# Order of the first operations of an attention-and-experts block: mixing weights, mask, table and gate rows

## The chip, the cores and the metric

The kernel runs on one core of a Trainium2 chip (trn2). A core has TensorE (matrix products, into PSUM), VectorE, ScalarE and GpSimd (elementwise work; each takes its instructions in order), and SyncE (SP), whose queue issues the transfers of this kernel. The metric is the time of one execution on the device, in microseconds (us). A profiled execution beside it gives the trace.

## What is computed

Three parts in a row, all in float32; the inputs are random and some are scaled. Cut to what matters:

```python
def _attn_ref(q, k, v, s):               # 4 batches, 8 heads, 576 rows, 64 wide
    cum = np.cumsum(np.maximum(s, 0.0), axis=-1)
    bias = -(cum[:, :, :, None] - cum[:, :, None, :])
    scores = np.where(causal, -1e9, q @ k.T / 8 + np.minimum(bias, 0.0))
    return softmax(scores) @ v

def _moe_ref(x, mu_k, mu_r, w_k, w_v, w_r):
    x_prev = shift(x)                    # the row before, zero for the first
    xk = mu_k * x + (1.0 - mu_k) * x_prev
    xr = mu_r * x + (1.0 - mu_r) * x_prev
    v = np.maximum(xk @ w_k, 0.0) ** 2 @ w_v
    return v / (1.0 + np.exp(-(xr @ w_r)))

def _moe2_ref(x, w_in, g_ln, w_sg, b_sg, w_out):
    u, v = split(gelu(x @ w_in))
    v_s = np.einsum('ts,bsd->btd', w_sg, layernorm(v) * g_ln) + b_sg
    return x + (u * v_s) @ w_out
```

## The kernel before

Attention goes in 20 jobs. A job is a pair of heads; the first batch's four pairs are cut into jobs 0 to 3 (query blocks 0 to 2) and 4 to 7 (blocks 3 and 4), all later pairs are one job each. Jobs 0 to 5 use the inputs in float32; later ones are split into two float32r halves. For each block a score product (`scores`, L344) goes to PSUM; VectorE (`fold`, L361, one custom instruction and one that reads its accumulator, nm) adds the mask, scales and finds the minimum; ScalarE makes the exponential (L387). In `rows` the result is transposed by TensorE (L422), copied by ScalarE (L424) and multiplied with v (L426, L430). The first block of each job (p0) has its own path: GpSimd multiplies it by the reciprocal of its sums (L438), TensorE transposes it (L440), ScalarE copies it (L442), TensorE multiplies it (L444). The finished heads stand in the tiles xt.

The second part (`moe1`) mixes each row with the row before: ScalarE multiplies by mu1, which is 1 - mu (L594), VectorE adds mu times the row (L600), ScalarE rounds to xh (L70) and GpSimd makes the rest xl (L73). The products with w_k, w_r and w_v follow (L661). Those weights come as raw 64-bit words and are converted on the chip (`convert`): ScalarE takes the absolute value (L110), VectorE does four integer steps (L114 to L117), ScalarE rounds (L70), VectorE makes the low half (L73). Eight parts of w_k, four of w_r and eight of w_v (512 KB each) are loaded, at most five ahead of their conversion; a load is held back by a small VectorE copy (L100) that stands for the buffer of an earlier conversion. The third part, after attention and the experts, is products with w_in, w_sg and w_out.

What sets the order: the program is written as generators that interleave the steps, with priorities (`tc.cur_priority`, lower goes first; FIRST, SECOND and THIRD move the beginning ahead), and a scheduler of the Tile framework turns priorities and its own estimate of times into one fixed order for each engine. On the chip the engines then follow their orders and wait for semaphores. A transfer of SP's queue stands in that order too.

At the beginning stand: the load of s (s_sb), the running sum cum (L264, L266), its copies into the extra rows of the first operand tile qk[0] (L269 to L272), constant rows of qk[0] and qk[1] (`rest`, L155), 14 matmuls of a tile of ones (L243), the identity (`make_identity`) and the mask (L250 to L263; mask0 is its form for p0), the rows cur for the other jobs (L277, L278), and gt, the float32r form of those rows, written to gate_d in DRAM for jobs 6 and later (L286 to L298). cur, gt and others live in the pool `cum`, which closes after gt; the tiles xt and the raw w_v are allocated behind that and may lie on its memory. The mixing weights come last:

```python
    mu_sb = const.tile([P, 2, 4], F32, name="mu_sb")
    nc.sync.dma_start(mu_sb, mu)
    mu1 = const.tile([P, 2, 4], F32, name="mu1")
    nc.gpsimd.tensor_scalar(mu1, mu_sb, -1.0, 1.0, ALU.mult, ALU.add)
```

Of the kernel before, what the change touches and what calls it, by code (L numbers as in the profile page):

```python
# [18 lines left out]
B, H, S, D = 4, 8, 576, 64  # L19
# [4 lines left out]
P = 128  # L24
NEG = -1.0e9
QS = [0, 64, 192, 320, 448]
QM = [64, 128, 128, 128, 128]
KN = [64, 192, 320, 448, 576]
PTW = 1408
C0, RATE, LEAD, AHEAD = 0.7, 1.1, 0.0, 5  # L30
FIRST = 100000
WARM = 14
SPLIT = 1
# [5 lines left out]
E1, ND, SECOND, THIRD = 2, 2, 5000, 1000  # L39
PA, PC, PM, PX = -1000, -500, -500, -500  # L40
NS, NV = 6, 8
PACE = 3
N0 = 8
ENG0 = {"qh": "DA", "ql": "P", "kh": "A", "kl": "D", "vh": "DA", "vl": "P"}
ENG = {"ia": "D", "mx": "D", "ca": "D", "p0": "P", "cl": "D", "qh": "D", "ql": "P", "kh": "A", "kl": "P", "vh": "A", "vl": "P", "xh": "A", "xl": "P", "fh": "D", "fl": "P", "rs": "D", "bh": "A", "bl": "D", "nh": "D", "nl": "D", "gh": "A", "gl": "D"}
MD = 320
# [5 lines left out]
def block_kernel(ctx: ExitStack, tc: tile.TileContext, qkv, vb, s, w_r, w_k, w_v, mu, w_in, w_out, w_sgT, g_ln, b_sg, out):  # L52
# [6 lines left out]
    nc = tc.nc  # L59
# [15 lines left out]
    const = ctx.enter_context(tc.tile_pool(name="const", bufs=1))  # L75
# [60 lines left out]
    ps_m = ctx.enter_context(tc.tile_pool(name="ps_m", bufs=2, space=PSUM))  # L136
# [10 lines left out]
    qk = [None, None]  # L147
# [6 lines left out]

    def rest(x, a, b, eng):  # L155

        eng.memset(qk[x][D:, 0, a:b], 8.0)
        nc.gpsimd.memset(qk[x][D:, 1, a:b], 0.0)
        nc.gpsimd.memset(qk[x][D : D + 1, 1, a:b], -8.0)

# [72 lines left out]
    gate_d = dram.tile([48, 2, 4, S], F32, name="gate_d")  # L233
    cur_d = dram.tile([48, S], F32, name="cur_d")
    cpool = tc.tile_pool(name="cum", bufs=1)
    cp = cpool.__enter__()
    if WARM:

        ones = cp.tile([P, 512], BF16, name="ones")
        nc.vector.memset(ones, 1.0)  # L240
        pm = ps_m.tile([P, 512], F32, tag="m", name="warm")
        for _ in range(WARM):
            nc.tensor.matmul(pm, ones[:, 0:P], ones, start=True, stop=True)  # L243
    zer = cp.tile([48, S], F32, name="zer")
    nc.gpsimd.memset(zer, 0.0)
    rest(0, S - KN[2], S + KN[2], nc.vector)
    rest(1, S - KN[2], S + KN[2], nc.vector)
    ident = const.tile([P, P], F32, name="ident")
    make_identity(nc, ident)
    mask = const.tile([P, 2 * MD + P], F32, tag="mask", name="mask")  # L250
# [9 lines left out]
    )  # L260
    mask0 = const.tile([P, P], F32, name="mask0")
    nc.vector.tensor_copy(mask0, mask[:, MD : MD + P])
    nc.vector.memset(mask0[D:, 0:D], 8.0 * NEG)  # L263
    nc.vector.tensor_scalar(s_sb, s_sb, 0.0, None, ALU.max)  # L264
    cum = cp.tile([48, S], F32, name="cum")
    nc.vector.tensor_tensor_scan(cum, s_sb, zer, 0.0, ALU.add, ALU.add)  # L266
    for i in (2, 1, 0):
        a, b, o = QS[i], KN[i], S - KN[i]
# [3 lines left out]
    nc.scalar.copy(qk[0][96:97, 1, S : S + KN[2]], cum[32:33, 0 : KN[2]])  # L272
    tc.cur_priority += FIRST - SECOND
    cur = cp.tile([48, S], F32, name="cur")
    for i in range(5):
# [4 lines left out]
    for x in range(2):  # L280
        for a, b in ((0, S - KN[2]), (S + KN[2], 2 * S)):
            rest(x, a, b, nc.gpsimd)
    for c in range(max(1, E1), AHEAD):
        load_words(wk, c % 4, c // 4, after=cur)
    tc.cur_priority += SECOND - THIRD
    gt = cp.tile([48, 2, 4, S], F32R, name="gt")  # L286
# [12 lines left out]
    cpool.__exit__(None, None, None)  # L299
    tc.cur_priority += THIRD  # L300


    mu_sb = const.tile([P, 2, 4], F32, name="mu_sb")
    nc.sync.dma_start(mu_sb, mu)
    mu1 = const.tile([P, 2, 4], F32, name="mu1")
    nc.gpsimd.tensor_scalar(mu1, mu_sb, -1.0, 1.0, ALU.mult, ALU.add)

    xtp = ctx.enter_context(tc.tile_pool(name="xtp", bufs=2))
    w1b = tc.tile_pool(name="w1b", bufs=1)
# [5 lines left out]
    def prepare(n, j):  # L315
        w = jobs[n]
        q, k, v = lds.pop((n, j))
        e = ENG0 if n < N0 else ENG
        if q is not None:
# [487 lines left out]
    for size in moe1():  # L807
# [17 lines left out]
        if att is None and w2 is None:  # L825
# [207 lines left out]
```

## Time and profile before

| | us |
|---|---|
| median of 3 runs | 714.64 (714.37 to 714.86) |
| profiled execution, whole | 712.34 |
| its span | 710.5 |
| TensorE busy | 670.2 (94%) |
| VectorE busy | 510.2 (72%) |
| ScalarE busy | 407.8 (57%) |
| GpSimd busy | 231.4 (33%) |

The span is what the trace shows, from the first instruction to the last; 1.8 us of the profiled execution lie around it. The granted clock is TensorE's, as a share of its full 2.4 GHz; 0.50 is the lower level of 1.2 GHz. The profile names PE (TensorE), PEld (its weight loads), DVE (VectorE), ACT (ScalarE), POOL (GpSimd), SP (SyncE). A busy time is an average over the stretch that it stands for.

### The profile page before, as it was taken

The numbers are of one execution on the slowest core, as the hardware profiler recorded it, in microseconds if no ns is written. First come the engines' busy times: TensorE is split into PE (matmuls) and PEld (weight loads), VectorE is DVE, ScalarE is ACT, GpSimd is POOL, SyncE is SP. The second block draws the span as 40 slices with busy tenths as digits, with TensorE's granted clock in tenths as the row PEclk, the third lists the DMA queues.
The fourth block names the chain that finished last, engine by engine and source line by source line (L and its number), as shares of the span: only waits on it lengthen the run. The fifth ranks groups of instructions, "written<-read, shape, count | busy, mean of one in ns | idle before, by whom it ended". The sixth has DMA issues, their size and how long they took to land.

```text
span 710.5 us, 12931 instructions
## 1 busy us (share of the span) xinstructions
PE 670.2 (94%) x4594; PEld 630.0 (89%) x4594; DVE 510.2 (72%) x1225; ACT 407.8 (57%) x978; POOL 231.4 (33%) x234
## 2 busy tenths in 40 slices
PE   6879979998999979999989999999999999999998
PEld 3657879987999969998989999999998998998998
DVE  8869998877878688779678598852946664664643
ACT  5759776877988867797777453633433133133120
POOL 7013553546655763576463073030000000000000
PEclk8779976999999999999999999999999999999999
DMA  9884542345244332424200630004230400300101
GB/s 242 238 253 145 155 123 56 95 125 159 73 128 141 89 107 57 143 85 119 89 22 21 204 131 29 6 18 142 78 117 3 131 3 5 129 1 5 63 1 68
DMA packets 39832, 67.48 MB, mean 95 GB/s; under 512 B 6908, under 2 KB 23400, under 8 KB 39736
## 3 DMA queue, kind: packets, MB, share of 16 engines
q1 hardware_dynamic: 39768, 66.66, 31.5%
q8 instruction: 36, 0.59, 0.3%
q14 instruction: 28, 0.23, 0.1%
HBM read 51.85 MB, written 10.19 MB: 87 GB/s over the span
## 4 chain that ended last, share of the span: by engine, by line
PE 71%; ACT 10%; DVE 10%; issue 3%; DMA 3%; POOL 1%; SPq 1%; DVEq 0%; ACTq 0%; POOLq 0%
PE m L661 25%; PE pu L674 7%; PE po L674 7%; PE av L511 3%; PE t L526 3%; PE pg L912 2%; PE pg L913 2%; ACT pr L387 2%; PE pg L911 2%; PE s L346 2%; PE av L430 2%; PE pv L848 2%; PE pv L849 2%; PE pv L850 2%; PE s L347 2%
## 5 line engine op out<-in xcount | busy, mean ns | idle before, releaser
L387 ACT ACTIVATE pr<-pr,nm 128x448 f32<-128x448 f32 (+4 forms) x144 | 85.3, 593 | 19.0 <-DVE nm L361 15.4
L73 POOL TENSOR_TENSOR xl<-xf,xh 128x288 fp32r<-128x288 f32 x64 | 69.0, 1091 | 79.5 <-ACT xh L70 40.5
L661 PE MATMUL m<-xh,wk 128*128 128x288 f32 x512 | 82.6, 300 | 0.0
L661 PE MATMUL m<-kh,wv 128*128 128x288 f32 x512 | 79.8, 297 | 0.0
L361 DVE CUSTOM_DVE_ANT_0 pr<-s,mask 128x288 f32<-128x288 f32 (+4 forms) x144 | 64.0, 454 | 15.6 <-PE t L526 6.4
L661 PEld LDWEIGHTS m<-xh,wk 128*128 128x128 f32 x512 | 73.0, 191 | 0.8
L661 PEld LDWEIGHTS m<-kh,wv 128*128 128x128 f32 x512 | 71.7, 188 | 0.5
L346 PE MATMUL s<-qk 128*128 128x288 f32 (+4 forms) x144 | 47.4, 330 | 12.2 <-DVE nh L361 7.7
L600 DVE SCALAR_TENSOR_TENSOR xf<-xt,mu_sb,xf 128x288 f32<-128x288 f32 x64 | 43.8, 688 | 12.4 <-ACT xf L594 12.2
L70 ACT CAST xh<-xf 128x288 fp32r<-128x288 f32 (+1 forms) x80 | 36.3, 482 | 24.2 <-DVE xf L600 13.5
L530 DVE TENSOR_TENSOR ptl<-t,pth 128x512 fp32r<-128x512 f32 (+1 forms) x72 | 44.1, 617 | 6.3 <-ACT pth L529 5.9
L661 PE MATMUL m<-xl,wk 128*128 128x288 f32 x256 | 48.1, 303 | 0.0
L594 ACT ACTIVATE xf<-xt,mu 128x288 f32<-128x288 f32 x64 | 33.9, 536 | 24.4 <-POOL xl L73 17.8
L529 ACT CAST pth<-t 128x512 fp32r<-128x512 f32 (+1 forms) x72 | 37.8, 532 | 15.6 <-PE t L526 15.0
L73 POOL TENSOR_TENSOR qk<-qld,qk 64x576 fp32r<-64x576 f32 (+1 forms) x28 | 38.9, 1389 | 20.3 <-DVE qk L70 4.3
L347 PE MATMUL s<-qk 128*128 128x288 f32 (+4 forms) x144 | 44.7, 313 | 0.0
L661 PE MATMUL m<-kl,wv 128*128 128x288 f32 x256 | 44.1, 299 | 0.0
L622 ACT ACTIVATE kf<-m 128x288 f32<-128x288 f32 x64 | 25.9, 410 | 30.6 <-PE m L661 28.9
L346 PEld LDWEIGHTS s<-qk 128*128 128x128 f32 x144 | 28.0, 194 | 16.4 <-DVE nh L361 9.1
L661 PE MATMUL m<-xh,wr 128*128 128x288 f32 x256 | 41.0, 301 | 1.3 <-ACT rt L635 1.0
L674 PE MATMUL pu<-xh,wi 128*128 128x288 f32 x256 | 40.6, 295 | 0.2 <-ACT ut L874 0.2
L70 ACT CAST gh<-gf 128x288 fp32r<-128x288 f32 x32 | 13.9, 435 | 46.0 <-DVE gf L918 46.0
(296 smaller groups left out, 1861.4 us busy)
## 6 DMA issues: line engine op xcount, KB each, us to landing
kld<-qkv SPq DMA_DIRECT2D x28, 288.0 KB
qld<-qkv SPq DMA_DIRECT2D x24, 288.0 KB
x_d<-rt SPq DMA_DIRECT2D x8, 576.0 KB
xf<-x_d SPq DMA_DIRECT2D x8, 576.0 KB
outT<-ot SPq DMA_DIRECT2D x32, 144.0 KB
vld<-qkv SPq DMA_DIRECT2D x24, 160.0 KB
qk<-qk SPq DMA_DIRECT2D x24, 144.0 KB
rb<-rd SPq DMA_DIRECT2D x24, 128.0 KB
```

Source lines behind the costliest of these rows:

```text
L70: nc.scalar.copy(dst, src) if eng == "A" else nc.vector.tensor_copy(dst, src)
L73: (nc.gpsimd if pick(engines) == "P" else nc.vector).tensor_tensor(dst, a, b.bitcast(F32), ALU.subtract)
L346: nc.tensor.matmul(dst, qk[0][:, 0, qs], qk[0][:, 1, ks], start=True, stop=False)
L347: issued[0] = nc.tensor.matmul(dst, qk[1][:, 0, qs], qk[1][:, 1, ks], start=False, stop=True)
L361: nc.vector.tensor_tensor_reduce(out=dst, in0=src, in1=msk, scale=-0.125, scalar=first, op0=ALU.add, op1=ALU.min, accum_out=acc)
L387: i = nc.scalar.activation(dst, dst, AF.Exp, bias=nm[:, col : col + 1], scale=-1.0, accum_out=w.sm[:, col : col + 1])
L529: nc.scalar.copy(pth[:, cols], bank[:, 0:o])
L530: nc.vector.tensor_tensor(ptl[:, cols], bank[:, 0:o], pth[:, cols].bitcast(F32), ALU.subtract)
L594: nc.scalar.mul(xf, xp, mu1[:, j, c : c + 1])
L600: nc.vector.scalar_tensor_tensor(xf, xc, mu_sb[:, j, c : c + 1], xf, ALU.mult, ALU.add)
L661: i = nc.tensor.matmul(dst, w(x, c, m), xx[:, c], start=(n + c == 0), stop=(n == 2 and c == w.nk - 1))
L674: nc.tensor.matmul(dst, w(x, c, m), xx[:, c], start=(n + c == 0), stop=(n == 2 and c == w.nk - 1))
```

## The change

The load of mu_sb is issued behind the first two loads of w_k, ahead of the rest of the program's beginning; mu1 stays where it was. The tiles xt get their memory before the pool `cum`. The memset matmuls are 18 with 384 columns instead of 14 with 512; their tile of ones is a constant. A one-column exponential of ones is ScalarE's first operation, so that its table is loaded there. `rest` takes the engine for its low rows as an argument: for the first columns of qk[0] that is VectorE, for all others GpSimd. The mask is made ahead of the identity and of qk[1]'s rows; mask0 comes after the first rows of cum. The priority of gt is later by GT = 300 than the code around it, and no longer earlier by THIRD.

```diff
-WARM = 14
+WARM = 18
+GT = 300
-    def rest(x, a, b, eng):
+    def rest(x, a, b, eng, low):
         eng.memset(qk[x][D:, 0, a:b], 8.0)
-        nc.gpsimd.memset(qk[x][D:, 1, a:b], 0.0)
-        nc.gpsimd.memset(qk[x][D : D + 1, 1, a:b], -8.0)
+        low.memset(qk[x][D:, 1, a:b], 0.0)
+        low.memset(qk[x][D : D + 1, 1, a:b], -8.0)
...
+    mu_sb = const.tile([P, 2, 4], F32, name="mu_sb")
+    nc.sync.dma_start(mu_sb, mu)
+    xtp = ctx.enter_context(tc.tile_pool(name="xtp", bufs=2))
     cpool = tc.tile_pool(name="cum", bufs=1)
...
+    ones = const.tile([P, 384], BF16, name="ones")
+    nc.vector.memset(ones, 1.0)
+    idle = ps_m.tile([P, 512], F32, tag="m", name="warm")
+    for _ in range(WARM):
+        nc.tensor.matmul(idle[:, 0:384], ones[:, 0:P], ones, start=True, stop=True)
+    first = const.tile([P, 1], F32, name="first")
+    nc.scalar.activation(first, ones[:, 0:1], AF.Exp)
...
-    rest(0, S - KN[2], S + KN[2], nc.vector)
-    rest(1, S - KN[2], S + KN[2], nc.vector)
-    ident = const.tile([P, P], F32, name="ident")
-    make_identity(nc, ident)
+    rest(0, S - KN[2], S + KN[2], nc.vector, nc.vector)
     mask = const.tile([P, 2 * MD + P], F32, tag="mask", name="mask")
...
-    mask0 = const.tile([P, P], F32, name="mask0")
-    nc.vector.tensor_copy(mask0, mask[:, MD : MD + P])
-    nc.vector.memset(mask0[D:, 0:D], 8.0 * NEG)
+    ident = const.tile([P, P], F32, name="ident")
+    make_identity(nc, ident)
+    rest(1, S - KN[2], S + KN[2], nc.vector, nc.gpsimd)
...
-    tc.cur_priority += SECOND - THIRD
+    tc.cur_priority += SECOND + GT
     gt = cp.tile([48, 2, 4, S], F32R, name="gt")
...
-    tc.cur_priority += THIRD
-    mu_sb = const.tile([P, 2, 4], F32, name="mu_sb")
-    nc.sync.dma_start(mu_sb, mu)
+    tc.cur_priority -= GT
```

The scheduler moves more than the diff says, as the orders of the two programs show (the number behind a name is a buffer's; in the changed kernel lines stand one or two further down). SP's queue from the loads of w_r to those of job 4 (qk 64x2x576), before:

```order
L101 DMA wr10w<-w_r 128x512
L208 DMA vld<-qkv 128x320 x2
L304 DMA mu_sb<-mu 128x8
L101 DMA wr20w<-w_r 128x512
L189 DMA qk_86<-qkv 64x2x576
L192 DMA qk_86<-cur_d 1x576
L193 DMA qk_86<-cur_d 1x576
L204 DMA vb<-vb 128x640
L189 DMA qk_86<-qkv 64x2x576
L192 DMA qk_86<-cur_d 1x576
L193 DMA qk_86<-cur_d 1x576
L101 DMA wr30w<-w_r 128x512
```

There mu_sb is behind the two loads of v (vld). SP's queue near its beginning now:

```order
L102 DMA wk00w<-w_k 128x512
L102 DMA wk10w<-w_k 128x512
L237 DMA mu_sb<-mu 128x8
L190 DMA qk_87<-qkv 64x2x320
L205 DMA vb<-vb 128x384
```

The load of mu_sb (L304 before, L237 now) stands behind the second of w_k. From wr10w on SP's queue reads now:

```order
L102 DMA wr10w<-w_r 128x512
L304 DMA gate_d<-gt 16x4608
L190 DMA qk_87<-qkv 64x2x320
L193 DMA qk_87<-cur_d 1x576
L194 DMA qk_87<-cur_d 1x576
L304 DMA gate_d<-gt 16x4608
L102 DMA wr20w<-w_r 128x512
L102 DMA wr30w<-w_r 128x512
L190 DMA qk_86<-qkv 64x2x576
L193 DMA qk_86<-cur_d 1x576
L194 DMA qk_86<-cur_d 1x576
L205 DMA vb<-vb 128x640
```

Both writes of gate_d (L304 now) stand here, the loads of v earlier, and the load of wr30w ahead of job 4's. GpSimd, from the reciprocal's users of jobs 0 and 1 (pr, L438 before and L440 now) to the first xl, before:

```order
L356 MEMSET sm 128x16
L438 TENSOR_SCALAR pr_305<-pr_305,rc 128x128
L356 MEMSET sm 128x16
L306 TENSOR_SCALAR mu_199<-mu_sb 128x8
L438 TENSOR_SCALAR pr_418<-pr_418,rc 128x128
L73 TENSOR_TENSOR xl<-xf,xh 128x288
L356 MEMSET sm 128x16
L73 TENSOR_TENSOR xl<-xf,xh 128x288
L438 TENSOR_SCALAR pr_542<-pr_542,rc 128x128
```

There mu1 (mu_199) is between the multiplies of jobs 1 and 2. GpSimd now, behind the memsets of gt:

```order
L295 MEMSET gt 48x576
L296 MEMSET gt 48x576
L309 TENSOR_SCALAR mu_208<-mu_sb 128x8
L440 TENSOR_SCALAR pr_219<-pr_219,rc 128x128
L358 MEMSET sm 128x16
L74 TENSOR_TENSOR xl<-xf,xh 128x288
L440 TENSOR_SCALAR pr_311<-pr_311,rc 128x128
L358 MEMSET sm 128x16
L440 TENSOR_SCALAR pr_424<-pr_424,rc 128x128
```

mu1 (mu_208 now) stands ahead of job 0's multiply, and the first xl ahead of job 1's. VectorE, behind the copies of cum (L269, L271), before:

```order
L271 COPY qk_86<-cum 1x320
L278 COPY cur<-cum 16x576
L100 COPY wk20w<-cur 48x1
L100 COPY wk30w<-cur 48x1
L100 COPY wk01w<-cur 48x1
L292 CAST gt<-cur 48x576
L114 TENSOR_SCALAR cvt<-cvt 128x512
L294 TENSOR_TENSOR gt<-cur,gt 48x576
L115 TENSOR_SCALAR cvt<-cvt 128x512
L262 COPY mask_142<-mask 128x128
L361 ISA pr_89,nm<-s,mask 128x320
L361 ISA nm 128x1
```

There the copy of the mask and the first fold (L361) come last. VectorE now, behind the same copies:

```order
L274 COPY qk_86<-cum 1x320
L278 COPY mask_164<-mask 128x128
L284 COPY cur<-cum 16x576
L279 MEMSET mask_164 64x64
L363 ISA pr_89,nm<-s,mask 128x320
L363 ISA nm 128x1
L363 ISA pr_88,nm<-s,mask 128x192
L363 ISA nm 128x1
L101 COPY wk20w<-cur 48x1
L101 COPY wk30w<-cur 48x1
L101 COPY wk01w<-cur 48x1
```

The first score's fold (L361 before, L363 now) stands ahead of the small copies, gt and the first conversion step. ScalarE keeps both absolute values (L110; wk00w and wk10w) and one cast of gt ahead of its first exponential. TensorE's order differs up to about the third of its instructions and is the same from there on.

## Rows read from the trace of the kernel before

**Rows 1.** The page, busy tenths in 40 equal slices of the span, and granted clock.

```profile
PE   6879979998999979999989999999999999999998
...
PEclk8779976999999999999999999999999999999999
```

**Rows 2.** Busy us by stretch (stretch, its length, engines with instruction counts, clock, DMA share, GB/s).

```profile
12.00:26.00 14.00, 12.32 (x46) 9.31 (x45) 12.20 (x41) 9.13 (x27) 2.94 (x14) 0.52 0.92 236
26.00:38.00 12.00, 8.69 (x53) 6.45 (x52) 10.72 (x41) 8.62 (x27) 0.85 (x2) 0.99 0.90 282
38.00:42.00 4.00, 0.15 (x2) 0.00 (x0) 0.77 (x4) 1.34 (x4) 0.77 (x2) 0.74 0.96 269
42.00:50.00 8.00, 7.76 (x29) 6.82 (x30) 6.00 (x22) 6.37 (x21) 2.33 (x4) 0.50 0.92 252
50.00:98.00 48.00, 42.02 (x286) 37.25 (x285) 47.09 (x114) 40.59 (x94) 21.55 (x21) 0.96 0.50 154
98.00:118.00 20.00, 17.34 (x77) 16.05 (x75) 19.53 (x39) 13.38 (x29) 10.55 (x8) 0.50 0.33 90
118.00:138.00 20.00, 20.00 (x155) 19.84 (x155) 16.03 (x40) 15.02 (x42) 10.03 (x12) 0.99 0.33 85
138.00:710.00 572.00, 555.19 (x3939) 531.42 (x3938) 388.94 (x912) 307.55 (x727) 171.44 (x145) 1.00 0.25 77
```

**Rows 3.** The chain of waits, 31 to 43 us: start us, us, what.

```profile
31.27 9.11 issue
...
40.43 0.21 POOL mu L306
...
41.10 0.52 ACT xf L594
...
42.23 0.45 PE t L440
```

**Rows 4.** Waits from 36 to 44 us: engine, line, waited for, us, times, longest.

```profile
POOL mu L306 <- DMA mu_sb<-mu: 9.2, 1, 9.2
ACT xf L594 <- POOL mu L306: 4.7, 1, 4.7
PEld t L440 <- POOL pr L438: 4.2, 1, 4.2
...
DVE xf L600 <- ACT xf L594: 3.6, 1, 3.6
```

**Rows 5.** Timeline around 40 us: start us, us, instruction, idle before and releaser.

```profile
36.22 0.43 SPq L304 DMA_DIRECT2D mu_sb<-mu  x1
...
37.66 0.49 PE L344 MATMUL s<-qk 128*128 128x128 f32 x2 [0.48 <-DVE nm L361]
...
43.55 0.80 POOL L73 TENSOR_TENSOR xl<-xf,xh 128x288 fp32r<-128x288 f32 x1 [2.36 <-ACT xh L70]
```

**Rows 6.** Timeline of the first 12 us.

```profile
1.59 1.26 DVE L157 MEMSET qk<- 64x640 f32 x2 [0.19 <-issue]
...
5.36 1.28 ACT L270 ACT_TABLE_LOAD   x1 [5.36 <-DVE cum L266]
...
6.34 1.58 POOL L159 MEMSET qk<- 1x640 f32 x2
...
10.74 0.67 ACT L110 ACTIVATE cvt<-wk10w 128x512 f32<-128x512 f32 x1 [0.75 <-DMA wk10w<-w_k]
...
11.11 0.47 DVE L361 CUSTOM_DVE_ANT_0 pr<-s,mask 128x320 f32<-128x320 f32 x1
...
11.70 1.04 PE L344 MATMUL s<-qk 128*128 128x128 f32 x4 [3.20 <-ACT cvt L110]
...
11.88 0.56 ACT L387 ACTIVATE pr<-pr,nm 128x320 f32<-128x320 f32 x1
```

**Rows 7.** Timeline 36 to 50 us: a load of job 4 and its scores.

```profile
37.22 0.61 SPq L189 DMA_DIRECT2D qk<-qkv  x1
...
49.41 1.03 PE L344 MATMUL s<-qk 128*128 128x288 f32 x2
```

More of the change, by code (lines that the diff above doesn't have):

```diff
@@ L234, in block_kernel @@
     cur_d = dram.tile([48, S], F32, name="cur_d")
+    mu_sb = const.tile([P, 2, 4], F32, name="mu_sb")
+    nc.sync.dma_start(mu_sb, mu)
+    xtp = ctx.enter_context(tc.tile_pool(name="xtp", bufs=2))
     cpool = tc.tile_pool(name="cum", bufs=1)
     cp = cpool.__enter__()
[L237 to L243, printed above, removed]
+    ones = const.tile([P, 384], BF16, name="ones")
[5 more added lines that the diff above has]
+    nc.scalar.activation(first, ones[:, 0:1], AF.Exp)
     zer = cp.tile([48, S], F32, name="zer")
     nc.gpsimd.memset(zer, 0.0)
-    rest(0, S - KN[2], S + KN[2], nc.vector)
-    rest(1, S - KN[2], S + KN[2], nc.vector)
-    ident = const.tile([P, P], F32, name="ident")
-    make_identity(nc, ident)
+    rest(0, S - KN[2], S + KN[2], nc.vector, nc.vector)
     mask = const.tile([P, 2 * MD + P], F32, tag="mask", name="mask")
@@ L273, in block_kernel @@
     tc.cur_priority += FIRST - SECOND
+    mask0 = const.tile([P, P], F32, name="mask0")
+    nc.vector.tensor_copy(mask0, mask[:, MD : MD + P])
+    nc.vector.memset(mask0[D:, 0:D], 8.0 * NEG)
     cur = cp.tile([48, S], F32, name="cur")
@@ L281, in block_kernel @@
         for a, b in ((0, S - KN[2]), (S + KN[2], 2 * S)):
-            rest(x, a, b, nc.gpsimd)
+            rest(x, a, b, nc.gpsimd, nc.gpsimd)
     for c in range(max(1, E1), AHEAD):
         load_words(wk, c % 4, c // 4, after=cur)
-    tc.cur_priority += SECOND - THIRD
+    tc.cur_priority += SECOND + GT
     gt = cp.tile([48, 2, 4, S], F32R, name="gt")
@@ L299, in block_kernel @@
     cpool.__exit__(None, None, None)
-    tc.cur_priority += THIRD
-    mu_sb = const.tile([P, 2, 4], F32, name="mu_sb")
-    nc.sync.dma_start(mu_sb, mu)
+    tc.cur_priority -= GT
     mu1 = const.tile([P, 2, 4], F32, name="mu1")
     nc.gpsimd.tensor_scalar(mu1, mu_sb, -1.0, 1.0, ALU.mult, ALU.add)
-    xtp = ctx.enter_context(tc.tile_pool(name="xtp", bufs=2))
     w1b = tc.tile_pool(name="w1b", bufs=1)
```

## The prediction

> **What bounds the kernel now.** I read the slices of the span first, then busy time by stretch, then the chain of waits, then the timeline around its largest hole. The slices [rows 1] show TensorE at nine tenths or more almost everywhere except in the first seven slices (some 125 us); the granted clock is below full there too. The stretches [rows 2] say it in numbers: from 118 us on TensorE is busy 20.00 of 20 and then 555.19 of 572 us, so what comes later is TensorE's own work and moves as a block: a microsecond saved before it is a microsecond off the end, as long as the order there stays good. Before it, from 50 to 118 us, VectorE is the full engine (47.09 of 48, then 19.53 of 20), with the weights' conversions; so a microsecond that VectorE gains before 50 us is passed on. The place where neither engine works is 38 to 42 us: TensorE 0.15, VectorE 0.77, ScalarE 1.34 of 4 us.
>
> The chain of waits [rows 3] runs through that hole: 9.11 us of "issue" from 31.27, then the one-minus-mu operation at 40.43, then the first mixing step on ScalarE, and at 42.23 TensorE's transpose of job 2's first block. The waits name the cause [rows 4]: GpSimd waited 9.2 us for the load of mu_sb, ScalarE 4.7 us for GpSimd, TensorE's weight load 4.2 us for GpSimd's pr (L438), VectorE 3.6 us. The timeline [rows 5] shows why: the 4 KB load is issued only at 36.22, behind weight and value loads, and GpSimd goes on at 40.43; job 2's L438 stands behind L306 on GpSimd, which works in order, and TensorE's transpose behind that. TensorE's last score matmuls before the hole start at 37.66 and take 0.49. So 38.15 to 42.23, 4.1 us, is a stall of everything.
>
> **The change part by part.**
>
> *The mixing weights first.* mu_sb goes from behind the two vld loads to right behind wk10w on SP's queue. In the trace wk10w has landed by 10.74 [rows 6], so 4 KB behind it are there long before L306 is due. That takes away the 9.2 us wait and with it TensorE's 4.1 us. What is late next there: L438 waits only for its reciprocal, as it did for the jobs before. VectorE loses 3.6 us less, ScalarE 4.7; I count TensorE's 4.1, which lies between. The 0.2 us of L306 itself and the later loads' 0.43 us of issue (all loads behind wk10w, beside work that the trace shows running) cost nothing that I can place; if that cover were gone, 0.4 us.
>
> *The clock behind the hole.* In 42 to 50 us the granted clock is 0.50, the lower level, 1.2 GHz, and TensorE is busy 7.76 of 8 us [rows 2]; before the hole, 26 to 38 us, it is 0.99 with TensorE busy 8.69 of 12 us. What TensorE did before the fall was nothing for 4 us. At full clock its 7.76 us would be 3.9, and then the busiest engine there is ScalarE with 6.37, VectorE having 6.00. So the stretch shrinks from 8 to 6.4 us at best, 1.6 us more, and by nothing if the clock falls anyway. I take 1.6, because 26 to 38 us is the same mix of work without the hole and kept its clock. The Trainium skill, "TensorE: Matmul & The Clock Gate", section "A second HAM failure mode: psum-queue depth-cycling", says that small idle times between groups of matmuls, without one long wait, can also make the clock swing; by it the 1.6 us would not come and the sum would be 4.1. The stretch from 26 to 38 us, 28% idle in small pieces at 0.99, speaks against it here.
>
> *Memsets moved to VectorE.* GpSimd loses one 64x640 and one 1x640 memset, VectorE gets both. On VectorE a 64x640 memset took 0.63 (1.26 for two), on GpSimd the 1x640 took 0.79 (1.58 for two) [rows 6]. The one on a single partition is not to be seen on VectorE: between nearly nothing and 0.63; I take 0.63, since on GpSimd one partition cost no less than VectorE's 64. The memset of ones gets a quarter shorter, some 0.1 us. So the running sum, whose end ScalarE waits for until 5.36 now, comes up to 0.63 + 0.63 - 0.1 = 1.1 us later. The Trainium skill, "VectorE: DVE Perf Modes", section "Zero memsets can be issued as uint32 (trn2)", has a memset take one cycle per element whatever the type, which speaks against the move, as it makes the single partition as dear as 64; by it the delay is the same 1.1 us, and no run here shows the single partition on VectorE.
>
> *ScalarE's table at once.* The 1.28 us load stands between the end of the running sum (5.36) and the copies that TensorE's first scores need [rows 6]. It goes to the start, where ScalarE is idle. Against the 1.1 us above that leaves 0.2 us.
>
> *Mask earlier, float32r rows later.* The first score in VectorE's row (L361) starts at 11.11, behind two gt operations, the first conversion steps and the copy of the mask; in the new order it comes right behind the copies of cum, some 2 us earlier. But ScalarE is in order: its first exponential (L387) stands behind the conversion of wk10w, which waits for that load until 10.74 [rows 6], and behind one cast of gt; both still stand ahead of it. 10.74 + 0.67 + 0.6 gives 12.0, against 11.88 now. So the earlier mask is worth nothing at first. Afterwards job 0's exponentials follow more closely, and its L440 comes ahead of job 1's scores instead of behind: job 0 earlier by 1 to 2 us, job 1's scores later. I take 0 for the whole front, between -1 and +2.
>
> *WARM.* 14 x 512 columns become 18 x 384, 6912 instead of 7168, 4% fewer, ahead of scores that wait for other things: nothing.
>
> *Loads moved.* wr30w (512 KB) goes ahead of job 4's loads, and both gate_d writes from 13.7 us to behind wr10w. The transfers are near their limit there (share 0.90 to 0.96 at 252 to 282 GB/s, 26 to 50 us [rows 2]), so 512 KB delays job 4 by up to 1.9 us. Job 4's first load is issued at 37.22 and its scores stand at 49.41 and shortly before [rows 7]; 5.7 us earlier there are still some 6 us between them, and the load of mu_sb, issued one microsecond before it, was there after 4.2 us (36.22 to 40.43). With 1.9 us more that makes 6.1. Between 0 and 1.9 us, then; I take 0, by that row.
>
> **Sum:** 4.1 + 1.6 + 0 + 0 = 5.7 us. The profiled execution took 712.34 us (span 710.5), so 706.6; the median of the runs is 714.64, 2.3 us above it, so **708.9 us**. With the bounds (gain 5.7 - 1 - 1.9 to 5.7 + 2) this case's own range is 706.9 to 711.8.
>
> **The rivals.**
>
> *The clock falls all the same* between 40 and 50 us, by the small idle times. Then 4.1 us: 710.5. Speaks for it: 12 to 26 us at 0.52 [rows 2], after a hole of 3.2 us ahead of 11.70 [rows 6]. Speaks against it: 26 to 38 us.
>
> *The long half-clock stretch goes as well.* From 98 to 118 us the clock is 0.50 while TensorE is busy 17.34 of 20 us, and from 118 to 138 us it is busy 20.00 of 20 [rows 2]: it has work in arrears. Ahead of it TensorE had waited for VectorE. A new order of the scores there (it differs up to the third of TensorE's instructions) may avoid that. At most 17.34 / 2 = 8.7 us, about half of it since VectorE is full there too: 700 to 704.6. Speaks against it: VectorE's load is unchanged.
>
> *The gain is lost on the way.* VectorE's full stretch and TensorE's half-clock stretch end together at 118 us; if the stretch gets longer by what came early, or job 4's loads are late, the time is within a microsecond of now: 713.3 to 716. A change that does not do what it says belongs here, but the order shows the load seventh on SP, so hardly.
>
> *A new hole, slower.* On GpSimd the p0 multiply of job 1 (L438) now stands behind the first xl (L73), which waits for ScalarE's cast, behind VectorE's mix, behind job 0's last copy: as the trace has it behind the hole, GpSimd waits 2.36 us for the cast and xl takes 0.80 [rows 5]; TensorE's transpose, now ahead of that job's products instead of behind, waits for it. A wait of up to 3.2 us alone costs less than the gain. It decides when it, or any later new gap, is followed by a half-clock stretch like that of 98 to 118 us: 8.7 us, more than the 5.7 + 1.4 needed to come out slower; 708.9 + 8.7 = 717.6.
>
> **How the numbers follow.** Forecast 0.45, clock falls all the same 0.13, long stretch gone 0.16, gain lost 0.13, new hole 0.13. About 0.2% (1.4 us) is what a measurement of this kernel can tell from no change, so faster means below 713.2: 0.45 + 0.13 + 0.16 = 0.74; the same 0.13; slower 0.13. The range leaves out the far half of the long-stretch case (0.08) and nearly all of the new hole (0.12): 702.5 to 715.
>
> **What would show it.** Right: no wait of GpSimd for mu_sb, L306 done before 20 us, no stall of all engines around 40 us; the clock at full between 36 and 46 us; job 4's first score near 43 us; from then to the end the same distances as now. First exponential within 0.5 us of 11.9. Wrong: TensorE's last half-clock stretch of the front ending at or after 118 us, TensorE waiting on L438 of job 1 for over 2 us, scores of job 4 waiting for their load, or a half-clock stretch after 130 us.

## The result and the profile after

The changed kernel takes **702.54 us** (median of 6, 701.33 to 703.45) against 714.5 for the kernel before (6 runs, 709.92 to 715.13): ratio 0.9844, 95% interval 0.9817 to 0.9871. It is 12.0 us faster; the forecast said 5.7 us, 708.9. The profiled execution has a span of 699.7 us, against 710.5. In the changed kernel most lines moved down by two: L306 is L309, L438 is L440, L440 is L442, L466 is L468, L600 is L602, L661 is L663; in the kernels of the experiments they stand up to two lines off again.

The page of the changed kernel, busy tenths and granted clock in 40 slices, to be laid beside [rows 1]:

```profile
PE   6888969999999989999899999999999999999998
...
PEclk8899968999999999999999999999999999999999
```

Its stretches beside [rows 2] (stretch, length, busy us of PE, PEld, DVE, ACT, POOL with counts, clock, DMA share, GB/s):

```profile
12.00:26.00 14.00, 10.33 (x41) 7.84 (x41) 13.13 (x40) 10.66 (x29) 3.08 (x5) 0.63 0.87 269
26.00:38.00 12.00, 8.98 (x49) 5.99 (x49) 12.00 (x43) 10.91 (x34) 1.61 (x3) 1.00 1.00 276
38.00:42.00 4.00, 3.94 (x22) 3.55 (x23) 3.55 (x13) 2.31 (x8) 1.82 (x3) 0.71 1.00 275
42.00:50.00 8.00, 5.80 (x31) 4.22 (x30) 6.29 (x23) 5.78 (x19) 1.18 (x1) 0.93 1.04 214
50.00:98.00 48.00, 39.52 (x273) 34.71 (x272) 47.90 (x107) 40.45 (x93) 24.64 (x22) 0.96 0.52 157
98.00:118.00 20.00, 18.43 (x104) 17.95 (x105) 15.85 (x41) 12.89 (x30) 8.17 (x8) 0.67 0.29 81
...
138.00:244.00 106.00, 103.07 (x749) 97.74 (x749) 87.64 (x222) 87.35 (x225) 64.75 (x54) 1.00 0.42 121
244.00:272.00 28.00, 26.10 (x180) 25.05 (x180) 23.31 (x54) 20.65 (x55) 16.98 (x19) 0.94 0.33 92
```

The hole at 38 to 42 us is gone (TensorE 3.94 of 4 us, 0.15 before), and 42 to 50 us runs at 0.93 and not at 0.50. The last two lines are a place that the forecast did not look at. Here is the kernel before in the same stretches:

```profile
138.00:244.00 106.00, 101.90 (x734) 95.38 (x734) 84.31 (x224) 86.33 (x223) 61.37 (x52) 1.00 0.40 117
244.00:272.00 28.00, 22.84 (x152) 21.23 (x151) 22.61 (x45) 20.64 (x53) 17.98 (x21) 0.94 0.28 80
```

TensorE stood 5.2 of the 28 us there, now 1.9, some 210 us behind the last edited operation, the second gate store (issued at 33.86 us).

The front in the changed kernel's timeline (start us, us, instruction, idle before and releaser), beside [rows 5, 6]:

```profile
0.73 1.28 ACT L249 ACT_TABLE_LOAD   x1 [0.73 <-PEq L1028]
...
2.81 0.59 DVE L158 MEMSET qk<- 64x640 f32 x1
...
4.07 0.59 DVE L160 MEMSET qk<- 1x640 f32 x1 [0.19 <-DVE s_sb L267]
...
11.09 0.66 ACT L111 ACTIVATE cvt<-wk10w 128x512 f32<-128x512 f32 x1 [1.81 <-DMA wk10w<-w_k]
...
12.21 0.56 ACT L389 ACTIVATE pr<-pr,nm 128x320 f32<-128x320 f32 x1
...
12.99 0.34 POOL L309 TENSOR_SCALAR mu<-mu_sb 128x8 f32<-128x8 f32 x1
...
44.76 0.72 PE L346 MATMUL s<-qk 128*128 128x288 f32 x2 [1.40 <-DMA qk<-qkv]
```

**Where the time went.** The products with w_k, w_r and w_v (L661 in the kernel before) have 1920 matmuls in every run here, in one order (but for two near 67 us in e2, f4 and h2). The start of one of them in a run, less its start in the profiled run of the kernel before, both from the start of the span, tells how far that run is ahead (minus) or behind (plus) at that point. The columns are the times of three such matmuls in the kernel before. "Same order" means that all four engines come to the changed kernel's order, by 138 us at the latest, and keep it; "old order" that TensorE comes to the order of the kernel before, by 165 us at the latest, and the other engines follow that order closely. From 279 us on (268 in the changed kernel) TensorE's order is the same in both kernels.

| kernel | at 141 us | at 288 us | at 498 us | order behind | profiled, us | median us |
|---|---|---|---|---|---|---|
| before, again | +1.2 | +1.2 | +2.0 | old | 714.49 | 714.63 |
| changed | -4.9 | -10.5 | -10.4 | its own | 701.49 | 702.54 |
| f1, weights at 24.9 us | -5.3 | -11.0 | -10.7 | same | 701.56 | 701.56 |
| f3, no early table | -7.2 | -13.0 | -12.9 | same | 699.56 | 701.49 |
| e3, gate rows old | -2.3 | -8.2 | -6.7 | same | 705.40 | 705.25 |
| h1, weights and gate rows old | -0.9 | -5.6 | -5.2 | same | 707.01 | 707.83 |
| f2, weights at 29.5 us | -1.8 | -6.5 | -5.9 | same | 706.44 | 707.65 |
| e1, early weights alone | +0.7 | +3.5 | +4.7 | old | 717.17 | 714.11 |
| h2, early weights and table | -1.5 | -4.0 | -4.0 | old | 708.73 | 709.74 |
| f4, mask's part undone | +7.3 | +4.1 | +4.3 | old | 716.33 | 720.15 |
| e2, all but the early weights | +4.1 | +7.5 | +9.1 | old | 721.25 | 717.46 |

Each row is one profiled run, and in e1, e2 and f4 that run lies 3 to 4 us off the median. Between 141 and 288 us every kernel with the changed kernel's order gains 4.7 to 5.9 us on the kernel before, whatever its front did; with the old order the change between the two is -3.2 to +3.5 us. Counted from the matmul at 162 us, by which TensorE has come to its later order in all of them, the gain is 4.6 to 5.0 us with the changed kernel's order, and with the old one 0 to 3.4 us are lost. Half of the result is made there.

What TensorE did up to the first of these matmuls, and from there to the second, each time in the kernel before and then in the changed one:

```profile
0.00:141.01 141.01, 117.79 (x677) 101.07 (x677) 123.96 (x321) 102.89 (x259) 60.90 (x91) 0.83 0.58 165
0.00:136.13 136.13, 113.06 (x680) 96.06 (x681) 123.32 (x326) 103.46 (x264) 62.45 (x90) 0.89 0.61 171
141.01:288.06 147.05, 138.02 (x983) 129.78 (x982) 115.96 (x294) 114.92 (x294) 85.89 (x76) 0.99 0.38 109
136.13:277.58 141.45, 136.62 (x983) 129.92 (x982) 116.89 (x291) 113.31 (x291) 87.24 (x76) 0.99 0.39 113
```

Up to the first, TensorE stands idle for 23.2 us before and 23.1 us now. The hole at 38 us is gone, but as much idle time stands in smaller pieces elsewhere: in 12 to 26, 42 to 50 and 50 to 98 us it was 1.7, 0.2 and 6.0 us, and is 3.7, 2.2 and 8.5. Of the 4.9 us of lead 4.7 are busy time, 117.8 against 113.1 us, at a mean granted clock of 0.83 and 0.89. Between the two matmuls it is mostly idle time that goes, 9.0 to 4.8 us, with 1.4 us of busy time, at a clock of 0.99 in both.

### The profile page after: what moved, and what is told of

Its sections match the earlier page's. It is cut to its first block, busy times and chain, and to the rows that moved or that the text cites. A ratio compares the mean times of both kernels' runs of the same rounds, so it can differ in the third digit from the quotient of the medians.

```text
span 699.7 us, 12939 instructions
## 1 busy us (share of the span) xinstructions
PE 663.8 (95%) x4598; PEld 624.9 (89%) x4598; DVE 510.3 (73%) x1227; ACT 406.5 (58%) x979; POOL 234.2 (33%) x232
## 4 chain that ended last, share of the span: by engine, by line
PE 69%; ACT 7%; DVE 6%; DMA 2%; issue 1%; SPq 1%; POOL 0%; DVEq 0%; ACTq 0%; POOLq 0%
PE m L663 26%; PE po L676 7%; PE pu L676 7%; PE av L513 3%; PE t L528 3%; PE pg L914 2%; PE pg L915 2%; PE pg L913 2%; PE pv L851 2%; PE pv L852 2%; PE pv L850 2%; ACT pr L389 2%; PE s L348 2%; PE s L349 2%; DVE xf L602 1%
## 5 line engine op out<-in xcount | busy, mean ns | idle before, releaser
L663 PE MATMUL m<-xh,wk 128*128 128x288 f32 x512 | 81.6, 298 | 0.0
L663 PE MATMUL m<-kh,wv 128*128 128x288 f32 x512 | 80.1, 297 | 0.0
L363 DVE CUSTOM_DVE_ANT_0 pr<-s,mask 128x448 f32<-128x448 f32 (+4 forms) x144 | 63.6, 453 | 17.3 <-PE s L349 8.9
L663 PEld LDWEIGHTS m<-xh,wk 128*128 128x128 f32 x512 | 71.9, 189 | 0.9
L663 PEld LDWEIGHTS m<-kh,wv 128*128 128x128 f32 x512 | 71.8, 189 | 0.6
L602 DVE SCALAR_TENSOR_TENSOR xf<-xt,mu_sb,xf 128x288 f32<-128x288 f32 x64 | 47.3, 744 | 6.5 <-ACT xf L596 6.1
L663 PE MATMUL m<-xl,wk 128*128 128x288 f32 x256 | 47.7, 299 | 0.0
L663 PE MATMUL m<-kl,wv 128*128 128x288 f32 x256 | 43.4, 299 | 0.0
L663 PE MATMUL m<-xh,wr 128*128 128x288 f32 x256 | 40.5, 300 | 1.2 <-ACT rt L637 0.9
L528 PE MATMUL t<-ident,pr 128*128 128x128 f32 x252 | 39.1, 276 | 0.4 <-DVE ptl L532 0.2
```

Of the source, the lines that this page charges most:

```text
L363: nc.vector.tensor_tensor_reduce(out=dst, in0=src, in1=msk, scale=-0.125, scalar=first, op0=ALU.add, op1=ALU.min, accum_out=acc)
L528: issued[0] = nc.tensor.transpose(bank[:, o : o + P], x, ident)
L602: nc.vector.scalar_tensor_tensor(xf, xc, mu_sb[:, j, c : c + 1], xf, ALU.mult, ALU.add)
L663: i = nc.tensor.matmul(dst, w(x, c, m), xx[:, c], start=(n + c == 0), stop=(n == 2 and c == w.nk - 1))
```

## The experiments

Ratios are to the kernel before, timed on the same chip (714.0 to 714.7 us in the three sets), with their 95% intervals.

**e1: the early weights alone.**

```
+    mu_sb = const.tile([P, 2, 4], F32, name="mu_sb")
+    nc.sync.dma_start(mu_sb, mu)
     cpool = tc.tile_pool(name="cum", bufs=1)
...
-    mu_sb = const.tile([P, 2, 4], F32, name="mu_sb")
-    nc.sync.dma_start(mu_sb, mu)
```

> The kernel before with one thing of the change, the load of the mixing weights behind wk10w. Theory A (the wait for that load was the front's loss; it and the half-clock stretch behind it are some 6 us; the other 4 to 5 us of the gain come from a stage around 250 us in which the order or the phase of the clock happened to fall well): no stall at 38 to 42 us, every later stage 4 to 6 us earlier, 708.5 to 710.5. Theory B (the whole 12 us follow from the wait): 702 to 704. Theory C (the other constants and the late gt rows carry most of it): 713 or more.

Measured: 714.11 us, 1.0012 (0.9991 to 1.0034). The part on which the whole forecast rested gives nothing alone. It is 3.0 us ahead at 55 us and 0.7 behind at 141; TensorE's order differs from that of the kernel before up to row 572 of 4478.

**e2: all of the change but the early weights**; their load goes from ahead of the mask to behind the gate rows, with a later priority.

```
-    nc.sync.dma_start(mu_sb, mu)
...
+    tc.cur_priority += 1500
+    nc.sync.dma_start(mu_sb, mu)
+    tc.cur_priority -= 1500
     mu1 = const.tile([P, 2, 4], F32, name="mu1")
```

> The changed kernel with the load of the mixing weights back behind wr10w, where it stood before. Theory A: the stall of all engines near 40 us is back, the front loses 4 to 6 us against the changed kernel: 706 to 709 if the later part keeps its gain, about 712 if that falls too. Theory B: 713 to 715. Theory C: 702 to 704.

Measured: 717.46 us, 1.0037 (1.0016 to 1.0059), slower than the kernel before. GpSimd's wait for the weights is back (7.7 us, until 37.27). From TensorE's row 353 on it has e1's order. So "change less weights" costs 15 us and "weights alone" gives none: the parts don't add up, since each set of edits makes the scheduler (the planner of the expectations) choose another order.

**e3: the gate rows made where they were.**

```
-    tc.cur_priority += SECOND + GT
+    tc.cur_priority += SECOND - THIRD
...
-    tc.cur_priority -= GT
+    tc.cur_priority += THIRD
```

> The changed kernel with the priority of the gt rows as before, so that both writes of gate_d go out ahead of most loads again. Theory A: within 2 us of the changed kernel, since nothing in the first 50 us waits for those transfers: 701 to 705. Theory C: 706 or more, because the loads of jobs 1 to 3 land some 2 us later behind 576 KB.

Measured: 705.25 us, 0.9874 (0.9848 to 0.99), 2.7 more than the changed kernel, with the same order on all four engines; only SP's queue differs. Waits of e3 on ScalarE, 26 to 38 us:

```profile
ACT cvt L111 <- DMA wk11w<-w_k: 2.0, 1, 2.0
```

and when e3 issues the stores and that load:

```profile
14.74 0.97 SPq L304 DMA_DIRECT2D gate_d<-gt  x2
23.05 0.65 SPq L102 DMA_DIRECT2D wk11w<-w_k  x1
```

The changed kernel issues wk11w at 19.69, with no such wait in 26 to 38 us. The two stores ahead of the key weights hold the conversion, and ScalarE's exponentials queue behind it. The clock there is 0.66 in e3, 1.00 in the changed kernel; but f1 below has 0.57 there and loses nothing, so that clock alone is not the price.

**e4: the kernel before once more**, unchanged.

> The kernel before, unchanged, for a second trace of it: its runs so far lie near 710 and near 714.6. Theory A: the two times differ in one stage around 250 us, and the first 150 us of the two traces agree within 1 us. If the difference is in the front instead, theory A's split of the gain is wrong.

Measured: 714.63 us, 1.0008 (0.9986 to 1.003). The profiled run is 1.1 us behind the first one at 55 us, 1.2 at 141 and 288, and 2.0 at 498 (table): between these two traces nothing arises where the changed kernel gains half of its time. The kernel's runs without a trace lie further apart (707.88 to 718.11 us over all sets), and where those differ no trace shows. The hole is not a fixed size either: GpSimd waits 9.7 us for the weights here, and TensorE's gap at its end is shorter (the first trace, then this one):

```profile
42.23 0.45 PE L440 MATMUL t<-ident,pr 128*128 128x128 f32 x1 [4.08 <-ACT p L424]
43.45 0.30 PE L440 MATMUL t<-ident,pr 128*128 128x128 f32 x1 [2.51 <-ACT p L424]
```

TensorE came to it later here, at a granted clock of 0.72 and not 0.99 from 26 to 38 us.

**f1: the changed kernel, weights behind wk11w.** All engines keep their orders but for one row: on GpSimd, L311 comes behind job 0's multiply (14.58 us) and the memset behind it, and not ahead of them.

```
+    tc.cur_priority += 99600
     nc.sync.dma_start(mu_sb, mu)
+    tc.cur_priority -= 99600
```

> The changed kernel, with the load of the mixing weights issued at the 28th place of SP's queue (behind the second group of key weights, wk11w) and not at the 7th; every row on PE, VectorE, ScalarE and GpSimd stands in the same order as in the changed kernel. By the landing of wk11w in the changed kernel's trace the weights should be there at 24 to 26 us, where GpSimd wants them at 13.0: its normalisation of job 0 (15.41 us there) and TensorE's first transpose of it (17.09 us) then wait some 8 to 10 us. Theory W (such a wait is carried to the end, whatever the order): 702.5 + 8 to 10 = 710.5 to 712.5. Theory D (up to 50 us the landings of weights and operands set the pace, TensorE is busy 9 of 12 us there, and take up part of a wait that ends by 27 us): 702.5 + 3 to 6 = 705.5 to 708.5, the shift at 30 us larger than at 60 us. I expect D, 707.

Measured: 701.56 us, 0.9825 (0.9801 to 0.9848): the same as the changed kernel. Neither W nor D is tested, since job 0's multiply, which both put behind the wait, stands ahead of it. GpSimd's timeline in f1, and ScalarE's first mix:

```profile
24.86 0.20 POOL L311 TENSOR_SCALAR mu<-mu_sb 128x8 f32<-128x8 f32 x1 [8.33 <-DMA mu_sb<-mu]
27.97 1.35 POOL L74 TENSOR_TENSOR xl<-xf,xh 128x288 fp32r<-128x288 f32 x1 [2.91 <-ACT xh L71]
...
25.09 0.53 ACT L598 ACTIVATE xf<-xt,mu 128x288 f32<-128x288 f32 x1 [1.19 <-POOL mu L311]
```

A wait of 8.33 us, almost the 9.2 of [rows 4], costs nothing that the end shows: the next operation on GpSimd is wanted only at 27.97, and ScalarE, which needs the result for its first mix, stands 1.19 us and comes to it 0.3 us later than in the changed kernel (24.78). The length of a wait says nothing without what is queued behind it.

**f2: the changed kernel, weights behind job 3's loads, orders the same from row 512 on** (the same edit with 99850).

> The changed kernel, with the load of the mixing weights issued behind the second group of key weights and job 3's loads, just ahead of the first receptance weight (34th place of SP's queue). Unlike the earlier run with the load behind the second receptance weight, the planner comes back to the changed kernel's order: all engines' rows are the same from TensorE's row 512 of 4478 on. The weights should land at 31 to 33 us, and GpSimd, which has the operation behind job 0's normalisation here, is held for 2 to 3 us ahead of job 1's (29.2 us in the changed kernel). Theory W (the wait alone): 702.5 + 2 to 4 = 704.5 to 706.5. Theory O (the planner's order behind the front decides most): no more than 1 to 4 as well, since the order behind is kept, so 703.5 to 706.5, and above all not the 717.5 of the run with the load further back. Over 710 would say that a late load costs by itself.

Measured: 707.65 us, 0.9917 (0.9891 to 0.9942), 5.1 over the changed kernel, past W's 706.5, and 10 us better than e2. Timeline in f2, GpSimd, then ScalarE and TensorE:

```profile
26.81 0.63 POOL L442 TENSOR_SCALAR pr<-pr,rc 128x128 f32<-128x128 f32 x1 [10.28 <-ACT pr L391]
29.51 0.20 POOL L311 TENSOR_SCALAR mu<-mu_sb 128x8 f32<-128x8 f32 x1 [2.08 <-DMA mu_sb<-mu]
...
29.75 0.53 ACT L598 ACTIVATE xf<-xt,mu 128x288 f32<-128x288 f32 x1 [1.92 <-POOL sm L360]
...
30.90 0.30 PE L444 MATMUL t<-ident,pr 128*128 128x128 f32 x1 [2.48 <-ACT p L428]
```

The wait is 2.08 us, and on GpSimd only a memset (L360) stands behind it. But ScalarE's first mix needs the result: ScalarE stands 1.92 us, until both are done, and starts the mix 5.0 us later than in the changed kernel; its copy of p comes behind that, and TensorE waits 2.48 us for the copy. So W is at work here by way of ScalarE. Of the 3.0 us by which f2 is behind the changed kernel at 141 us, the share of the wait and that of the other order of TensorE's rows 71 to 512 can't be told apart. Afterwards f2 gains 4.7 us, as h1 does.

**f3: without the early table.**

```
-    first = const.tile([P, 1], F32, name="first")
-    nc.scalar.activation(first, ones[:, 0:1], AF.Exp)
```

> The changed kernel without the early one-column exponential on ScalarE, all other rows of all engines in the same order; ScalarE's table is loaded at its first copy of the cumulated gate (about 6 us), and not at 0.7 us. Forecast's own reading (the first exponential waits for the conversion of wk10w, which lands at about 11 us): 702.5, within 1. Rival: the 1.28 us of the load come onto the chain of the first fold: 703.5 to 704.

Measured: 701.49 us, 0.9831 (0.9806 to 0.9856). The early table is worth nothing, as the forecast had it.

**f4: the mask's part undone**: identity and both constant blocks ahead of the mask, mask0 right behind it.

```
-    rest(0, S - KN[2], S + KN[2], nc.vector, nc.vector)
+    rest(0, S - KN[2], S + KN[2], nc.vector, nc.gpsimd)
+    rest(1, S - KN[2], S + KN[2], nc.vector, nc.gpsimd)
+    ident = const.tile([P, P], F32, name="ident")
+    make_identity(nc, ident)
     mask = const.tile([P, 2 * MD + P], F32, tag="mask", name="mask")
...
+    mask0 = const.tile([P, P], F32, name="mask0")
```

> The changed kernel with the mask's part undone: identity ahead of the mask, both constant blocks ahead of it, the constant rows on GpSimd, mask0 right behind. The mixing weights stay early, the table at once, the gate rows late. The planner then comes to the order of the run with the early weights alone (the same from TensorE's row 697 of 4478 on), not to that of the changed kernel. Theory W (the gain is the early weights): 702.5 + 0 to 1.5. Theory O (the order that the planner finds behind the front holds some 4 to 9 us): 706.5 to 712, with the difference arising behind 60 us and not in the front.

Measured: 720.15 us, 1.01 (1.0074 to 1.0127), worse than O's 712. It is 10.2 us ahead of the kernel before at 55 us, the furthest of all, and 9.5 behind at 127. VectorE in f4:

```profile
51.68 0.15 DVE L101 COPY wv00w<-cvt 128x1 f32<-128x1 f32 x1 [6.40 <-DMA gate_d<-gt]
```

The first value weight takes the gate rows' memory. VectorE came to it before the late store had read them, and stood 6.40 us, from 45.3 on.

**h1: the kernel before with mask, table and warm-up of the change; weights and gate rows where they were.** From the changed kernel, the load (and the pool xtp) goes back behind the gate rows, and e3's edit is made:

```
-    nc.sync.dma_start(mu_sb, mu)
...
-    tc.cur_priority += SECOND + GT
+    tc.cur_priority += SECOND - THIRD
...
+    nc.sync.dma_start(mu_sb, mu)
     mu1 = const.tile([P, 2, 4], F32, name="mu1")
```

> The kernel before with the mask's part (mask ahead of identity, one set of constant rows on VectorE, mask0 later) and the table at once; the mixing weights are loaded where they were (behind the second receptance weight), the gate rows made where they were. GpSimd has the operation on the mixing weights between job 1's and job 2's normalisation, as in the kernel before, and should wait for it to about 40 us, as there. The planner's order behind the front is that of the changed kernel (the same from TensorE's row 512 of 4478 on). Theory W (the gain is the wait removed): 713 to 715, no gain. Theory O (the gain is mostly the order behind the front): 702.5 + 2.7 (the gate rows' old place, from the run with that alone) + up to 4 (the wait) = 705 to 709.5. I expect O, 707.

Measured: 707.83 us, 0.992 (0.9902 to 0.9939); O's 707. The wait is still there, and ends a microsecond earlier than in [rows 3]:

```profile
39.44 0.20 POOL L308 TENSOR_SCALAR mu<-mu_sb 128x8 f32<-128x8 f32 x1 [7.42 <-DMA mu_sb<-mu]
```

and still 244 to 272 us looks like the changed kernel's 26.10, not like 22.84:

```profile
244.00:272.00 28.00, 25.14 (x183) 23.72 (x182) 24.33 (x54) 22.11 (x59) 18.13 (x22) 1.00 0.30 84
```

At 141 us h1 is 0.9 us ahead of the kernel before, less than the 1.2 by which that kernel's two traces differ; at 288 us it is 5.6 ahead. The 4.7 us between are the share of the order behind the front by itself.

**h2: f4 with the gate rows where they were** (e3's edit on f4).

> The run with the mask's part undone, and the gate rows also where they were: of the change only the early mixing weights and the table at once are left. In the run with the mask undone VectorE stood 6.4 us (45.3 to 51.7 us) for the store of the gate rows, whose memory the first value weight takes over. Theory G (that wait made it slower than the kernel before): 712.5 to 715.5, as the early weights alone (714.1), and no such wait in the trace. Theory O alone (the order behind the front, which both share): 718 to 721.

Measured: 709.74 us, 0.9941 (0.9924 to 0.9958). VectorE's wait is gone, as G said, and 10.4 us with it, more than G gave. So the later gate rows gain 2.7 us in one order (e3) and cost 10.4 in another, with the part of TensorE's order, up to 149 us, that differs between f4 and h2. From 244 to 272 us TensorE is busy 22.84 of 28 here too.

**h3: what holds TensorE up at 244 to 272 us.** The kernel before, in the place where it idles; VectorE first, then GpSimd:

```profile
249.61 3.01 DVE L600 SCALAR_TENSOR_TENSOR xf<-xt,mu_sb,xf 128x288 f32<-128x288 f32 x1
...
262.34 3.84 DVE L466 TENSOR_SCALAR sm<-sm 128x9 f32<-128x9 f32 x1
```

```profile
261.81 1.43 POOL L73 TENSOR_TENSOR qk<-kld,qk 64x576 fp32r<-64x576 f32 x1
263.19 0.09 POOL L716 MEMSET xt<- 128x1 f32 x1
263.25 1.55 POOL L73 TENSOR_TENSOR xl<-xf,xh 128x288 fp32r<-128x288 f32 x2
264.77 1.39 POOL L492 TENSOR_TENSOR xt<-xt,rb 128x576 f32<-128x576 f32 x1
```

An addition to 128x9 elements takes 3.84 us: it ends at 266.18, with the last of a row of GpSimd operations (266.16). Over all its 12 instances in the kernel before (minimum, median, maximum in ns):

```profile
L466 DVE TENSOR_SCALAR sm<-sm x12: 160/586/3843, 135.4 to 378.3; 128x9 f32<-128x9 f32 x12
```

VectorE works in order, so the folds behind it come late, and TensorE with them (waits, 246 to 272 us):

```profile
PE s L346 <- DVE nh L361: 2.9, 1, 2.9
...
PE av L511 <- DVE ptl L530: 2.2, 1, 2.2
```

In the changed kernel the mix is held for 2.60 us in this place (and a later one takes 1.59, at 253.23), and the addition not at all:

```profile
243.91 2.60 DVE L602 SCALAR_TENSOR_TENSOR xf<-xt,mu_sb,xf 128x288 f32<-128x288 f32 x1
...
252.80 0.17 DVE L468 TENSOR_SCALAR sm<-sm 128x9 f32<-128x9 f32 x1 [0.85 <-ACT pr L389]
```

The profiled runs of e1, e2, e4, f4 and h2 have the 3.0 us (at 246 to 255 us) and the 3.8 us (at 257 to 268 us) as the kernel before has them, and a 3.65 to 3.69 us one at 168 to 177 us (173.26 in the kernel before); no run with the changed kernel's order has an addition of over 2.75 us. The experiment leaves the addition of 1e-9 out of the kernel before (and out of the result) and keeps the orders of ScalarE, GpSimd and SP, and TensorE's but for eight rows:

```
-        (nc.gpsimd if pick(ENG["ia"]) == "P" else nc.vector).tensor_scalar(w.sm[:, cols], w.sm[:, cols], 1e-9, None, ALU.add)
         nc.vector.reciprocal(rcp[:, cols], w.sm[:, cols])
```

> The kernel before without the addition of 1e-9 to the row sums of the later jobs (one VectorE operation of 128x9 for each job, left out of the computation); all rows of ScalarE, GpSimd and SP keep their order, VectorE's but for the rows left out, and TensorE's but for its rows 527 to 534. In the trace of before that operation takes 0.16 us where GpSimd is idle, and 3.65 us at 173 us, 3.84 us at 262 us and 2.75 us at 355 us, beside two or three GpSimd operations that follow one another; TensorE waits 2.2 us behind the first two. Theory P (VectorE's form is kept out while GpSimd works, and the reciprocal behind it is not): those three stalls go, 714.4 - 3 to - 6 = 708.5 to 711.5. Rival R (whatever stands there is kept out, and the reciprocal takes the 3 to 4 us over): 713.5 to 715.

Measured: 705.4 us, 0.9888 (0.9863 to 0.9914), beyond P's 708.5. The reciprocal in its place does not take the time over:

```profile
L466 DVE RECIPROCAL rcp<-sm x12: 198/210/217, 133.9 to 372.2; 128x9 f32<-128x9 f32 x12
```

In the trace h3 gains 2.8 us between 162 and 184 us, where a 3.65 us instance stood at 173.26, but only 0.7 us at 249 to 272: there another operation (L640, 128x1152) now meets the same GpSimd row and takes 3.51 us. In the third place a cast of VectorE (L70, at 350.64) takes 2.45 us, 0.45 where GpSimd is idle. P is right on the form; of R the reciprocal's part is wrong, but in two places of three the next held form behind it takes most of the time over. The spans of the profiled runs differ by 5.7 us, the medians by 8.6; 1.7 of the 5.7 arise before 141 us, where only the first of the twelve additions has run, and what makes up the rest of the 8.6 I did not find.

**h4: the same in the changed kernel** (1e-9 left out).

> The changed kernel without the same addition of 1e-9 (left out of the computation). Its own trace has only one such stall on that operation, 2.75 us at 345 us, with TensorE working on beside it, so theory P gives 702.5 - 0 to - 1.5 as far as the stalls go; but the planner's order differs from the changed kernel's between TensorE's rows 538 and 1480, and theory O says that this can cost or give 4 us by itself: 698 to 707. I expect 702.

Measured: 700.39 us, 0.9816 (0.9799 to 0.9833), some 2 us under the changed kernel, with overlapping intervals, and with another order between TensorE's rows 538 and 1480. So it does not tell the addition's share in the changed kernel from the order's.

## Why the prediction was right in sign and half in size

The measured 702.54 us lies outside the forecast's own range (706.9 to 711.8) and inside 702.5 to 715 by 0.04 us. That lower end came from the rival of the long half-clock stretch, which is not what gave the time: there the range held by luck.

**The stall and its cause: right.** No wait for mu_sb is left on GpSimd, L309 runs at 12.99 (forecast: before 20), and TensorE has no hole near 40 us. **Its price, 4.1 + 1.6 us: wrong in kind.** The step that failed is "I count TensorE's 4.1": it took the idle time of one place in one run for a gain at the end. TensorE is idle as long as before up to the same matmul (23.1 against 23.2 us), and of the lead there, 4.9 us, 4.7 are busy time, at a higher granted clock, for which the forecast had 1.6. Even in the kernel before the gap was 4.08 us in one trace and 2.51 in the other (e4), and the run with the smaller gap was not ahead. In e1 the wait is gone and the clock from 42 to 50 us is 1.00, and nothing is gained; in f1 a wait of 8.33 us cost nothing; in f2 one of 2.08 us held up ScalarE and TensorE. e3 and h1 differ in the wait and in the order up to TensorE's row 512, and both together are 1.4 us at 141 us, 2.6 in the medians. What the wait costs in the old order by itself no run shows: each earlier load changed that order. With h1's order the same wait leaves TensorE 2.36 us of work in 38 to 42 us, not 0.15.

**The front at 0: right.** First exponential at 12.21, forecast 12.0, held by wk10w's load as said; 1x640 on VectorE 0.59, forecast 0.63; f3 shows the table worth nothing.

**The loads moved at 0, a cost if anything: wrong sign.** The later gate stores gave 2.7 us (e3) by letting the key weights in earlier. I looked at who is pushed back (job 4, whose scores do wait 1.40 us for their load, a sign of being wrong by the forecast's own list) and not at who moves up.

**"What comes later moves as a block": the step that failed most.** It had the condition "as long as the order there stays good", and took the old order for good. The share of 118 us to the end was high (555.19 of 572), but the 17 us not busy were not TensorE's own: 5.2 of them lie at 244 to 272 us, and the order that the scheduler made of the new front takes 3.3 of these away. Order behind the front: 5.6 us (table, 141 to 288 us), 4.7 in h1 alone.

Summed from the profiled runs at 141 us: rest of the front (h1) 0.9, wait with its order 1.4, gate stores 2.6, which is 4.9; then the order 5.6, which is 10.5 at 288 us. That the 4.9 us of the front are close to the forecast's 5.7 is luck: they come from other terms than it said.

**The rivals.** The clock falls near 40 us all the same, but for less long: 38 to 42 us has 0.71 (0.74 before) and 42 to 50 us 0.93 (0.50 before), so the sign "the clock at full between 36 and 46 us" did not come. The long half-clock stretch got shorter and did not go: 98 to 118 us has 0.67 and not 0.50, but of the 6.1 us that the changed kernel is ahead at 88 us, 4.8 are left at 127. The new hole behind job 1's L440 did not come; from 8 to 36 us the longest wait for L440 is 1.3 us.

**Open:** which single row of the front turns the scheduler to the better order (f4 shows that the mask's part is needed beside the early weights, h1 that it does without the weights and the gate rows, e2 that it is not enough with late weights and late gate rows); which part of the front raised TensorE's clock; and why f4 loses 19.6 us between 55 and 127 us, of which VectorE's 6.40 is only a part: h2, without that wait, loses 12.1 us between 88 and 127. Part of f4's loss is other work done earlier: at the matmul at 141 us TensorE has begun 700 matmuls and not 677, four of them warm-up, and 4.3 us come back by 162.

## What to carry to other kernels

Where a scheduler sets the order, an edit's own saving is only one term: compare the orders far behind the edit, and look there for places where the engine that sets the pace idles, since a new order may heal or make them. Price a wait by what is queued behind it, on its own engine and on those that need its result, never by its length: 8.33 us cost nothing (f1), and 2.08 us held up ScalarE and TensorE (f2). Before an idle stretch is counted as a gain, compare idle time, busy time and clock up to the same instruction in both kernels: here the hole went and the idle time stayed. And read minimum against maximum of small operations: 160 ns and 3843 ns for one line says that something else holds it.

## What was not expected of the hardware

Some VectorE operations stand still while GpSimd works: a 128x9 addition took 0.16 us alone, 3.65 and 3.84 us beside three and four GpSimd operations in a row; the mix of two buffers (L600, 0.47 to 3.01) and the operation on 128x1152 (0.74 to 3.51) too. The reciprocal from the same buffer (198 to 217 ns in 12 instances, one of them at 171.54 us, inside a GpSimd operation from 170.82 to 172.44) and the folds, whose scores come from PSUM, did not. The Trainium skill, "SBUF — State Buffer", section "Who interferes with whom", says that VectorE in its two-port modes (copies, casts, tensor_scalar), or with two SBUF inputs against a GpSimd instruction that reads SBUF, shares a port pair with GpSimd by an exclusive lock for a whole instruction. The traces agree on which forms are held, and show more than one instruction's length: 3.84 us, until the whole row of GpSimd operations was through.

A memset of one partition by 640 took the same 0.59 us on VectorE as one of 64 partitions.
